# Retention scores of a chunk packed into three quarters of their block, with key halves swapped for every second head pair

## The chip, the cores and the metric

The kernel runs on one core of one Trainium2 chip. The metric is device time in microseconds, from three timed runs; beside them stands one profiled execution, whose trace the rows below come from.

## The reference

Decayed attention ("retention") over 4 batches of 8 heads, 576 tokens and head width 64, then two feed-forward layers (512 to 2048 to 512), the first with a leaky ReLU, the second with a squared ReLU:

```python
scores = scale * np.matmul(q, k.transpose(0, 1, 3, 2))
gamma = 1.0 - 2.0 ** (-5.0 - np.arange(H, dtype=np.float32))
rel = pos[:, None] - pos[None, :]
Dmat = np.where(rel >= 0, gamma[:, None, None] ** rel[None, :, :], 0.0)
ret = scores * Dmat[None, :, :, :]
x = np.matmul(ret, v)              # -> (B*S, H*D)
h = x @ w_in;  g = np.maximum(0.01 * h, h);  x = g @ w_out      # first layer
h = np.maximum(x @ w_in, 0.0);  out = h * h @ w_out             # second layer
```

A score whose key comes after its query is multiplied by zero.

## The kernel before

The retention part cuts each batch into four chunks of 128 tokens and one of 64 (20 chunks, numbered 0 to 19; chunks 4, 9, 14 and 19 are the short ones, chunks 0, 5, 10 and 15 open a batch). Inside a chunk the scores are formed and multiplied with V; what earlier chunks contribute comes through a running state. For each chunk `i` the program writes, in this order on each engine's queue:

- `load` and `load_rows`: q, k transposed (`kt`), and k and v by rows (`kv`) come in through SyncE's DMA queue, four chunks ahead, into five buffers each.
- `scores` (L515), two chunks ahead of the output: for a full chunk 16 matmuls of 64 x 64 weights by 128 columns into PSUM `scps` (two buffers); then VectorE multiplies all 128 x 1024 numbers by the decay mask (L518) into `r`. Scores of chunk i+2 need the buffer that L518 of chunk i reads.
- `decay`: GpSimd scales q (L531) and k (L535).
- `output`: the state product (L549, from the second chunk of a batch on), the within-chunk product of `r` and v (L557, 8 matmuls of 128 rows by 128 columns), ScalarE's copy of `ops` into `ysb` (L560), the sums that update the state (L566), and ScalarE's copy of the sums into `state` (L570), which the next chunk's state product reads.

Between chunks, `run` and `build` put work for the feed-forward part into the same queues, by the written tables RATE and BUILD: VectorE and ScalarE unpack weights (`steps_in`, `steps_out`, L149 to L216) and prepare the operands of the first layer (`operands`, L256 to L281). Into the last three chunks go the first products of that layer (L318). Behind the retention part the feed-forward layers follow, with matmuls of 128 x 128 weights by 384 or 512 columns (L318, L419), and VectorE and ScalarE beside them. All orders are written by hand (`manual_schedule`); each engine works through its queue in order.

Of the kernel before, what the change touches and what calls it, by code (L numbers as in the profile page):

```python
# [10 lines left out]
F32 = mybir.dt.float32  # L11
F32R = mybir.dt.float32r
U32 = mybir.dt.uint32
AF = mybir.ActivationFunctionType
# [3 lines left out]
B, H, S, D = 4, 8, 576, 64  # L18
NT, DM, DFF = B * S, H * D, 2048
P = 128  # L20
NP = H // 2
# [5 lines left out]
HT = 384  # L27
NB = NT // (2 * HT)
FULL = S // P
C = NP * P  # L30
# [12 lines left out]
AHEAD = 2  # L43
# [7 lines left out]
def retention_ffn_kernel(ctx: ExitStack, tc: tile.TileContext, full, rows, half, halfv, w1, w2, const, mask, gk, out):  # L51
# [12 lines left out]
    nc = tc.nc  # L64
    sub, mul, add, mx = ALU.subtract, ALU.mult, ALU.add, ALU.max
# [7 lines left out]
    ysb = [keep.tile([P, NK * 2 * HT], F32, name=f"ysb{i}") for i in range(NB)]  # L73
# [32 lines left out]
    class Weights:  # L106


        def __init__(self):
            self.tasks = []  # L110
            for g in range(2 * NG):
                layer, f = divmod(g * GRP, NF)
                a, b, c, d = ((j, layer, f + 2 * u) for j in range(2) for u in range(NU))

                self.tasks += [a, c, d, b] if g else [a, b, c, d]
            self.raws, self.loads = [], 0
            self.clock, self.due, self.arrive = 0, 0, 0
            self.free, self.later = False, True
# [320 lines left out]
    def halves_of(t0, n):  # L439
        for i in range(2 * NB):  # L440
            a, z = max(t0, i * HT), min(t0 + n, (i + 1) * HT)
            if a < z:
                yield i, a, z

    def tokens(i):
        b, c = chunks[i]
        return b * S + c * P, P if c < FULL else S - FULL * P

    class Retention:
        def __init__(self, pool, outputs):  # L450
# [52 lines left out]
        def scores(self, i):  # L503

            q, k = self.raw[i][:2]
            n = tokens(i)[1]

            ps = wide(i % 2, "scps").rearrange("p j (a t) -> p j a t", t=P)
            for p in range(NP):
                c = slice(p * n, (p + 1) * n)  # L510
                for f in range(0, n, D):
                    for j in range(2):
                        s = slice(j * D, (j + 1) * D)
                        o = slice(f, f + D) if n == P else s
                        nc.tensor.matmul(ps[o, j, p, :n], k[s, c][:, f : f + D], q[s, c], start=True, stop=True, skip_group_check=True)  # L515
# [4 lines left out]
            for j in range(2):  # L520
                s = slice(j * D, (j + 1) * D)
                nc.vector.tensor_tensor(t[s, j, :, :n], ps[s, j, :, :n], self.mask[s, j, :, j * D : j * D + n], mul)

        def decay(self, i):

# [6 lines left out]
            if c < FULL:  # L532
                k = kv[:, 0, :].rearrange("p (h e) -> p h e", e=D)
                g = self.gk[:, c].unsqueeze(2).to_broadcast([P, H, D])
                nc.gpsimd.tensor_tensor(k, k, g, mul)  # L535

        def output(self, i):
            q, _, kv = self.raw.pop(i)
            rs = self.r.pop(i)
            t0, n = tokens(i)  # L540
            c = chunks[i][1]
            ops = self.ops[:, :, i % 2]
            for p in range(0, NP if c > 0 else 0, 2):
# [6 lines left out]
            for p in range(0, NP, 2):  # L550
                for e in range(4):
                    j, h = e // 2, e % 2
                    a = p + h
                    s = slice((2 * a + j) * D, (2 * a + j + 1) * D)
                    o = ops[h * D : (h + 1) * D, j, p // 2, :n]
                    f = slice(0, P) if n == P else slice(j * D, (j + 1) * D)
                    nc.tensor.matmul(o, kv[f, 1, s], rs[f, j, a, :n], start=(c == 0 and p == 0), stop=(p == NP - 2), skip_group_check=True)  # L557
            for i, a, z in halves_of(t0, n):
                x = ysb[i // 2].rearrange("p (j s t n) -> p j s t n", j=2, s=2, t=2)[:, :, :, i % 2, a - i * HT : z - i * HT]
                nc.scalar.activation(x, ops[:, :, :, a - t0 : z - t0], AF.Copy)  # L560
            if c < FULL:

                for p in range(NP):
                    for j in range(2):
                        s = slice((2 * p + j) * D, (2 * p + j + 1) * D)
                        nc.tensor.matmul(  # L566
                            self.sums[j * D : (j + 1) * D, p], kv[:, 0, s], kv[:, 1, s],
                            start=(c == 0 and p == 0), stop=(c == FULL - 1 and p == NP - 1), skip_group_check=True,
                        )
                nc.scalar.activation(self.state, self.sums, AF.Copy)  # L570


    weights = Weights()
# [26 lines left out]
    with tc.manual_schedule():  # L600
        with tc.tile_pool(name="att", bufs=1) as pool, tc.tile_pool(name="outputs", bufs=1, space=PSUM) as outputs:
            att.append(Retention(pool, outputs))
            ret = att[0]
            n = len(chunks)
# [19 lines left out]
            for i in range(n):  # L624
# [15 lines left out]
                a, t = tokens(i)  # L640
# [81 lines left out]
def constants():  # L722

    gamma = (1.0 - 2.0 ** (-5.0 - np.arange(H, dtype=np.float32))).astype(np.float64)
    scale = 1 / np.sqrt(D)
    row, col = np.arange(P)[:, None], np.arange(C)[None, :]
    gq = [gamma[row // D + 2 * (col // P)] ** (c * P + col % P) * scale for c in range(1, FULL + 1)]
    since = col % P - row
    mask = [np.where(since >= 0, gamma[2 * (col // P) + j] ** np.maximum(since, 0) * scale, 0) for j in range(2)]
    gk = gamma ** -(np.arange(FULL)[:, None] * P + row[:, :, None]).astype(np.float64)  # L730
    return [a.astype(np.float32) for a in (np.stack(gq), np.concatenate(mask, axis=1), gk.reshape(P, -1))]


# [45 lines left out]
```

## Time and profile before

| | |
|---|---|
| three timed runs | 842.29, 838.79, 840.78 us; median 840.78 us |
| the profiled execution | 841.1 us, of which 839.3 us span |
| busy in the span: TensorE, VectorE, ScalarE, GpSimd | 813.3, 603.4, 333.4, 44.4 us |
| mean granted TensorE clock | 0.992 |

The span runs from the first to the last instruction; the time of an execution also holds what lies around it, 1.8 us here. An engine's busy time overlaps with that of the others. GpSimd works in the retention part only.

### The profile page before, as it was taken

To read this page: it belongs to the slowest core of one execution; us is meant where nothing else is said; L and a number is where in the kernel's file an instruction comes from. 1 tells how busy PE (TensorE), PEld (TensorE's weight loads), DVE (VectorE), ACT (ScalarE), POOL (GpSimd) and SP (SyncE) were. 2 spreads that over 40 slices of the span, in tenths; PEclk is the share of its full clock that TensorE was granted. 3 is DMA by queue.
4 is the path that set the end of the run, shared out by engine and by line. 5 is a ranking of instruction groups with operands and counts; after the bars stand their busy time and mean duration, and the time that the engine had idled before them with its cause. 6 is when DMAs were issued, how large, how long until landed. Compare 5 with 4: busy or idle time off the path is not lost.

```text
span 839.3 us, 13140 instructions
## 1 busy us (share of the span) xinstructions
PE 813.3 (97%) x5468; PEld 767.1 (91%) x5468; DVE 603.4 (72%) x737; ACT 333.4 (40%) x431; POOL 44.4 (5%) x36
## 2 busy tenths in 40 slices
PE   7887999999999999999999999999999999999998
PEld 6777899999999999999999998998998998998996
DVE  4897889657666566658668879868778778754534
ACT  1344656544523433524525365443422333321211
POOL 3853000000000000000000000000000000000000
PEclk9998999999999999999999999999999999999999
DMA  9987473966656737746823554966855756745711
GB/s 360 393 311 278 150 276 121 420 244 243 259 175 243 255 135 288 263 134 243 302 99 132 182 226 164 390 246 228 299 174 205 265 169 243 263 145 193 289 51 75
DMA packets 45947, 191.58 MB, mean 228 GB/s; under 512 B 5696, under 2 KB 6720, under 8 KB 45888
## 3 DMA queue, kind: packets, MB, share of 16 engines
q1 hardware_dynamic: 45456, 189.96, 60.9%
q8 instruction: 43, 0.70, 0.3%
q10 hardware_dynamic: 432, 0.79, 0.3%
q14 instruction: 16, 0.13, 0.0%
HBM read 152.98 MB, written 37.75 MB: 227 GB/s over the span
## 4 chain that ended last, share of the span: by engine, by line
PE 82%; DVE 8%; DMA 5%; ACT 2%; issue 2%; SPq 0%; ACTq 0%; DVEq 0%
PE yps L419 44%; PE a L318 21%; PE b L318 15%; DMA kt<-in_full 2%; DMA raw<-in_w 1%; DMA gq<-in_const 1%; ACT sf L149 1%; DMA kv<-in_rows 1%; DVE sf L205 1%; DVE ilo L187 1%; PE ops L557 1%; DVE x L260 1%; DVE r L518 1%; DVE t L370 0%; DVE sf L209 0%
## 5 line engine op out<-in xcount | busy, mean ns | idle before, releaser
L318 PE MATMUL a<-x,ihi 128*128 128x384 f32 x768 | 196.0, 336 | 2.8 <-DVE t L384 2.5
L318 PE MATMUL b<-x,ihi 128*128 128x384 f32 x576 | 146.5, 335 | 0.8 <-DVE t L370 0.8
L318 PEld LDWEIGHTS a<-x,ihi 128*128 128x128 f32 x768 | 138.4, 188 | 5.9 <-DVE t L384 4.0
L419 PE MATMUL yps<-ghi,ohi 128*128 128x384 f32 x384 | 128.6, 335 | 1.0 <-ACT ysb L428 1.0
L318 PE MATMUL a<-x,ilo 128*128 128x384 f32 x384 | 128.5, 335 | 0.0
L419 PE MATMUL yps<-ghi,olo 128*128 128x384 f32 x384 | 128.3, 334 | 0.0
L419 PE MATMUL yps<-glo,ohi 128*128 128x384 f32 x384 | 128.3, 334 | 0.0
L356 DVE TENSOR_TENSOR glo<-t,ghi 128x768 fp32r<-128x768 f32 x96 | 91.7, 956 | 45.8 <-ACT ghi L351 45.2
L430 DVE TENSOR_TENSOR ysb<-yps,ysb 128x384 f32<-128x384 f32 (+1 forms) x126 | 76.1, 611 | 61.2 <-PE yps L419 60.9
L419 PE MATMUL yps<-ohi,glo 128*128 128x512 f32 x288 | 112.3, 390 | 0.0
L419 PE MATMUL yps<-olo,ghi 128*128 128x512 f32 x288 | 112.3, 390 | 0.0
L419 PE MATMUL yps<-ohi,ghi 128*128 128x512 f32 x288 | 112.0, 389 | 0.0
L351 ACT ACTIVATE ghi<-t 128x768 fp32r<-128x768 f32 x96 | 81.1, 845 | 68.5 <-DVE t L329 55.1
L318 PEld LDWEIGHTS b<-x,ihi 128*128 128x128 f32 x576 | 103.7, 188 | 1.6 <-DVE t L370 1.1
L344 ACT ACTIVATE s<-a 128x768 f32<-128x768 f32 x47 | 38.2, 814 | 155.3 <-PE a L318 155.2
L318 PE MATMUL b<-x,ilo 128*128 128x384 f32 x288 | 96.3, 334 | 0.0
L419 PEld LDWEIGHTS yps<-ghi,ohi 128*128 128x128 f32 x384 | 72.1, 188 | 1.9 <-ACT ysb L428 1.3
L419 PEld LDWEIGHTS yps<-glo,ohi 128*128 128x128 f32 x384 | 72.1, 188 | 0.0
L419 PEld LDWEIGHTS yps<-ghi,olo 128*128 128x128 f32 x384 | 72.1, 188 | 0.0
L318 PEld LDWEIGHTS a<-x,ilo 128*128 128x128 f32 x384 | 72.1, 188 | 0.0
L419 PEld LDWEIGHTS yps<-ohi,glo 128*128 128x128 f32 x288 | 54.0, 188 | 11.3
L419 PEld LDWEIGHTS yps<-olo,ghi 128*128 128x128 f32 x288 | 54.0, 188 | 11.0
(67 smaller groups left out, 976.2 us busy)
## 6 DMA issues: line engine op xcount, KB each, us to landing
x<-x SPq DMA_DIRECT2D x168, 768.0 KB, 6.0
raw<-in_w SPq DMA_DIRECT2D x62, 512.0 KB, 5.9
kv<-in_rows SPq DMA_DIRECT2D x16, 512.0 KB, 6.0
out<-ysb SPq DMA_DIRECT2D x18, 256.0 KB, 2.0
q<-in_full SPq DMA_DIRECT2D x16, 256.0 KB, 5.2
kt<-in_full SPq DMA_DIRECT2D x13, 256.0 KB, 5.1
ysb<-in_w SPq DMA_DIRECT2D x2, 512.0 KB, 6.7
kv<-in_halfv SPq DMA_DIRECT2D x4, 256.0 KB, 5.6
```

Of the source, the lines that this page charges most:

```text
L149: nc.scalar.activation(f32(a), f32(raw[:, :, 1]), AF.Abs)
L187: nc.vector.tensor_tensor(lo[:, a:z], sf[:, a + 1 : z + 1], f32(hi[:, a:z]), sub)
L205: nc.vector.scalar_tensor_tensor(rest, high, 23, low, ALU.logical_shift_left, ALU.bitwise_or)
L260: nc.vector.tensor_tensor(t[:, 1], src, f32(t[:, 0]), sub)
L318: nc.tensor.matmul(ps[:, u, :HT], a[:, w, s], x[:, b, k], start=(start and k == 0 and i == 0), stop=(k == 1 and i == 2), skip_group_check= ...
L344: nc.scalar.activation(t, ps[:, :, :HT], AF.Copy)
L351: nc.scalar.activation(h, t, AF.Copy)
L356: nc.vector.tensor_tensor(l, t, f32(gs[key][0]), sub)
L419: nc.tensor.matmul(acc, a, b, start=(j == u == i == 0), stop=(j == 1 and u == NU - 1 and i == 2))
L430: nc.vector.tensor_tensor(y, acc, y, add)
L518: nc.vector.tensor_tensor(t, ps, self.mask, mul)
L557: nc.tensor.matmul(o, kv[f, 1, s], rs[f, j, a, :n], start=(c == 0 and p == 0), stop=(p == NP - 2), skip_group_check=True)
```

## The change

Of a chunk's 128 x 128 scores per head, the quarter of first-half queries by second-half keys is all zero after the mask. `scores` no longer multiplies it: keys of the first half meet all 128 queries (8 matmuls of 128 columns), keys of the second half only the 64 late ones (8 matmuls of 64 columns). So that three blocks of 64 columns hold two heads without a hole, every second head pair (`odd`) has its key halves swapped: its early keys stand in partitions 64 to 127. The host swaps the halves in `kv` alike, and mask and `gk` follow. The mask product is one VectorE operation on 128 x 768 numbers (L540), and a short chunk's mask is a tile of its own (`tail`), with a DMA of its own.

The within-chunk product falls into two: `within(1)`, late queries with all 128 keys (8 matmuls of 64 columns), and `within(0)`, early queries with 64 early keys (8 matmuls of 64 columns, of which even pairs use rows and output partitions 0 to 63 and odd pairs 64 to 127). `within(1)` stays ahead of the sums, `within(0)` goes behind them, and so does the copy of `ops` to `ysb`, which now follows the copy of the state. Ahead of either part a new matmul of 2 columns (`fence`) is put, in chunks that are neither the first nor the last of a batch.

```diff
-            self.mask = pool.tile([P, 2, NP, P], F32, name="mask")
+            self.mask = pool.tile([P, 2, NP // 2, 3 * D], F32, name="mask")
+            self.tail = pool.tile([P, NP, D], F32, name="tail")
...
-            nc.sync.dma_start(self.mask.rearrange("p j a t -> p (j a t)"), mask)
+            nc.sync.dma_start(self.mask.rearrange("p j a t -> p (j a t)"), mask[:, : -C // 2])
+            nc.sync.dma_start(self.tail.rearrange("p a t -> p (a t)"), mask[:, -C // 2 :])
...
-            t = self.r[i] = self.pool.tile([P, 2, NP, P], F32, tag="r", bufs=1 + AHEAD, name="r")
-            if n == P:
-                nc.vector.tensor_tensor(t, ps, self.mask, mul)
...
+            for a in range(NP // 2):
+                for late in range(2):
+                    for j in range(2):
+                        s = slice(j * D, (j + 1) * D)
+                        for odd in (late, 1 - late):
+
+                            c = (2 * a + odd) * P
+                            f = (late ^ odd) * D
+                            o = ps[f : f + D, j, a, 1 + odd] if late else ps[f : f + D, j, a, : 2 + odd : 1 + odd]
+                            x = q[s, c + late * D : c + P].rearrange("p (b t) -> p b t", t=D)
+                            nc.tensor.matmul(
+                                o, k[s, c + late * D : c + late * D + D], x[:, 0] if late else x,
+                                start=True, stop=True, skip_group_check=True,
+                            )
+            m = self.mask.rearrange("p j a c -> p j (a c)")
+            t, ps = (x.rearrange("p j a b t -> p j (a b t)") for x in (t, ps))
+            nc.vector.tensor_tensor(t, ps, m, mul)
...
+        def fence(self):
+
+            ps = bank("fence", 3)
+            nc.tensor.matmul(ps[:D, :2], self.cold[:D, :D], self.cold[:D, :2], start=True, stop=True)
...
-                    nc.tensor.matmul(o, kv[f, 1, s], rs[f, j, a, :n], start=(c == 0 and p == 0), stop=(p == NP - 2), skip_group_check=True)
-            for i, a, z in halves_of(t0, n):
-                x = ysb[i // 2].rearrange("p (j s t n) -> p j s t n", j=2, s=2, t=2)[:, :, :, i % 2, a - i * HT : z - i * HT]
-                nc.scalar.activation(x, ops[:, :, :, a - t0 : z - t0], AF.Copy)
+
+            def within(part):
+                for a in range(NP // 2):
+                    for e in range(4):
...
+                        elif part:
+                            f = slice(0, P)
+                            x, o = rs[:, j, (3 * a + 1 + h) * D : (3 * a + 2 + h) * D], o[:, D:]
+                        else:
+                            f = slice(h * D, (h + 1) * D)
+                            x, o = rs[f, j, 3 * a * D : (3 * a + 1) * D], o[:, :D]
...
+            if 0 < c < FULL:
+                self.fence()
+            within(1)
             if c < FULL:
...
                 nc.scalar.activation(self.state, self.sums, AF.Copy)
+                if c > 0:
+                    self.fence()
+                within(0)
+            for i, a, z in halves_of(t0, n):
+                x = ysb[i // 2].rearrange("p (j s t n) -> p j s t n", j=2, s=2, t=2)[:, :, :, i % 2, a - i * HT : z - i * HT]
+                nc.scalar.activation(x, ops[:, :, :, a - t0 : z - t0], AF.Copy)
```

TensorE's queue at chunk 18, the last full one, before the change: state product, within-chunk product, sums, and the first products of the feed-forward part (`a`, `b`).

```order
L549 MATMUL ops<-q,state 64x128 x8
L557 MATMUL ops<-r,kv 64x128 x8
L566 MATMUL sums<-kv 64x64 x8
L318 MATMUL b<-x,ihi 128x384 x2
L318 MATMUL b<-x,ilo 128x384
```

The same place after the change (L572 is the state product, L590 the two parts of the within-chunk product, L600 the sums):

```order
L572 MATMUL ops<-q,state 64x128 x8
L558 MATMUL fence<-cold 64x2
L590 MATMUL ops<-r,kv 64x64 x8
L600 MATMUL sums<-kv 64x64 x8
L558 MATMUL fence<-cold 64x2
L590 MATMUL ops<-r,kv 64x64 x8
L318 MATMUL b<-x,ihi 128x384 x2
L318 MATMUL b<-x,ilo 128x384
```

Two fences have come in, and half of the within-chunk product stands behind the sums.

ScalarE's queue around chunks 14 to 16 before the change: the copies of chunk 14 (64 columns), the weight step L212, then the copies of chunk 15 (`ysb`, `state`) and of chunk 16.

```order
L560 ACTIVATE ysb_68<-ops 128x4x64
L212 ACTIVATE ohi<-sf 128x1024
L560 ACTIVATE ysb_68<-ops 128x4x128
L570 ACTIVATE state<-sums 128x256
L560 ACTIVATE ysb_68<-ops 128x4x64 x2
L570 ACTIVATE state<-sums 128x256
```

And after the change:

```order
L610 ACTIVATE ysb_68<-ops 128x4x64
L212 ACTIVATE ohi<-sf 128x1024
L604 ACTIVATE state<-sums 128x256
L610 ACTIVATE ysb_68<-ops 128x4x128
L604 ACTIVATE state<-sums 128x256
L610 ACTIVATE ysb_68<-ops 128x4x64 x2
```

In each full chunk the copy of the state now stands ahead of the copy of the output. VectorE's, GpSimd's and SyncE's queues keep their order, but for the DMA of `tail` behind that of `mask`.

## Rows read from the trace of the kernel before

**Rows 1.** Busy time by stretch: engines in us, TensorE's granted clock, DMA share, GB/s.

```profile
0.00:35.30 35.30, 26.21 (x560) 23.07 (x562) 22.37 (x22) 9.96 (x16) 18.47 (x17) 0.95 0.98 380
35.30:71.70 36.40, 27.90 (x692) 24.78 (x690) 36.11 (x34) 13.56 (x25) 24.16 (x18) 0.91 0.82 286
71.70:85.60 13.90, 13.90 (x217) 12.35 (x217) 8.10 (x10) 7.34 (x13) 1.80 (x3) 0.86 0.89 350
85.60:130.00 44.40, 42.01 (x237) 40.12 (x234) 37.90 (x46) 27.42 (x38) 0.00 (x0) 1.00 0.52 190
130.00:839.30 709.30, 703.26 (x3777) 666.75 (x3775) 498.95 (x628) 275.15 (x339) 0.00 (x0) 1.00 0.59 218
```

**Rows 2.** Chain that ended last, from 20 to 75 us: start, us, what.

```profile
23.74 7.27 DMA kt<-in_full
...
34.08 1.20 ACT sf L149
...
68.55 1.14 DVE sf L209
...
70.68 0.58 ACT ysb L560
71.26 0.28 ACT state L570
...
71.68 1.13 PE ops L549 x16
```

**Rows 3.** TensorE's waits up to 86 us: total, times, longest.

```profile
PE scps L515 <- DVE r L518: 6.5, 4, 2.6
```

**Rows 4.** VectorE's groups by line and shape: count, busy us, mean ns, idle before.

```profile
L370 DVE TENSOR_TENSOR t<-b,s 128x768 f32<-128x768 f32 x24 | 23.0, 956 | 55.5 <-PE b L318 55.4
...
L518 DVE TENSOR_TENSOR r<-scps,mask 128x1024 f32<-128x1024 f32 x16 | 19.3, 1214 | 7.1 <-DMA mask<-in_mask 5.3 <-PE scps L515 1.8
...
L207 DVE TENSOR_SCALAR sf<-sf 128x1024 uint32<-128x1024 uint32 x16 | 12.0, 753 | 0.0
```

**Rows 5.** VectorE in order of time, 33 to 75 us: start, us, what.

```profile
36.53 1.21 DVE L518 TENSOR_TENSOR r<-scps,mask 128x1024 f32<-128x1024 f32 x1
...
65.66 1.76 DVE L207 TENSOR_SCALAR sf<-sf 128x1024 uint32<-128x1024 uint32 x1
67.34 1.21 DVE L518 TENSOR_TENSOR r<-scps,mask 128x1024 f32<-128x1024 f32 x1
```

**Rows 6.** TensorE in order of time, 19 to 23 us.

```profile
19.18 1.10 PE L515 MATMUL scps<-q,kt 64*64 64x128 f32 x32
20.11 0.62 PE L549 MATMUL ops<-q,state 64*64 64x128 f32 x16
20.66 1.09 PE L557 MATMUL ops<-r,kv 128*64 128x128 f32 x16
21.58 0.63 PE L566 MATMUL sums<-kv 128*64 128x64 f32 x16
22.14 0.68 PE L515 MATMUL scps<-q,kt 64*64 64x64 f32 x16
```

**Rows 7.** TensorE in order of time, 43 to 45 us.

```profile
44.13 0.41 PE L549 MATMUL ops<-q,state 64*64 64x64 f32 x16
```

**Rows 8.** Waits of TensorE's weight loads, 13 to 86 us: total, times, longest.

```profile
PEld ops L557 <- issue: 2.7, 14, 0.3
```

**Rows 9.** TensorE in order of time, from 71 us.

```profile
72.74 1.97 PE L557 MATMUL ops<-r,kv 128*64 128x128 f32 x16
74.50 1.07 PE L566 MATMUL sums<-kv 128*64 128x64 f32 x16
```

**Rows 10.** ScalarE in order of time, from 65 us.

```profile
82.31 0.60 ACT L560 ACTIVATE ysb<-ops 128x512 f32<-128x512 f32 x1 [0.77 <-PE ops L557]
...
83.11 1.57 ACT L256 ACTIVATE x<-ysb 128x768 fp32r<-128x768 f32 x2
```

**Rows 11.** TensorE's waits, 85 to 480 us: total, times, longest.

```profile
PE b L318 <- DVE t L370: 0.8, 1, 0.8
```

More of the change, by code (lines that the diff above doesn't have):

```diff
@@ L506, in scores @@
             n = tokens(i)[1]
[L508 to L511, printed above, removed]
+            ps = wide(i % 2, "scps")
+            t = self.r[i] = self.pool.tile([P, 2, NP // 2 * 3 * D], F32, tag="r", bufs=1 + AHEAD, name="r")
+            if n < P:
+                ps, t = (x[:, :, : NP * n].rearrange("p j (a t) -> p j a t", t=n) for x in (ps, t))
+                for p in range(NP):
+                    c = slice(p * n, (p + 1) * n)
@@ L520, in scores @@
-            for j in range(2):
-                s = slice(j * D, (j + 1) * D)
-                nc.vector.tensor_tensor(t[s, j, :, :n], ps[s, j, :, :n], self.mask[s, j, :, j * D : j * D + n], mul)
+                        nc.tensor.matmul(ps[s, j, p], k[s, c], q[s, c], start=True, stop=True, skip_group_check=True)
+                for j in range(2):
+                    s = slice(j * D, (j + 1) * D)
+                    nc.vector.tensor_tensor(t[s, j], ps[s, j], self.tail[s], mul)
+                return
@@ L549, in output @@
                     nc.tensor.matmul(o, self.state[s, a], q[s, a * n : (a + 1) * n], start=(p == 0), stop=False, skip_group_check=True)
[L550 to L556, printed above, removed]
-                    nc.tensor.matmul(o, kv[f, 1, s], rs[f, j, a, :n], start=(c == 0 and p == 0), stop=(p == NP - 2), skip_group_check=True)
-            for i, a, z in halves_of(t0, n):
-                x = ysb[i // 2].rearrange("p (j s t n) -> p j s t n", j=2, s=2, t=2)[:, :, :, i % 2, a - i * HT : z - i * HT]
-                nc.scalar.activation(x, ops[:, :, :, a - t0 : z - t0], AF.Copy)
+            def within(part):
+                for a in range(NP // 2):
+                    for e in range(4):
+                        j, h = e // 2, e % 2
+                        s = slice((4 * a + 2 * h + j) * D, (4 * a + 2 * h + j + 1) * D)
+                        o = ops[h * D : (h + 1) * D, j, a]
+                        if n < P:
+                            f = slice(j * D, (j + 1) * D)
+                            x, o = rs[f, j, (2 * a + h) * D : (2 * a + h + 1) * D], o[:, :n]
+                        elif part:
[4 more added lines that the diff above has]
+                            x, o = rs[f, j, 3 * a * D : (3 * a + 1) * D], o[:, :D]
+                        first = c == 0 and a == 0 and part == 1
+                        nc.tensor.matmul(o, kv[f, 1, s], x, start=first, stop=(a == NP // 2 - 1), skip_group_check=True)
+            if 0 < c < FULL:
+                self.fence()
+            within(1)
             if c < FULL:
@@ L727, in constants, with decay @@
     gq = [gamma[row // D + 2 * (col // P)] ** (c * P + col % P) * scale for c in range(1, FULL + 1)]
-    since = col % P - row
-    mask = [np.where(since >= 0, gamma[2 * (col // P) + j] ** np.maximum(since, 0) * scale, 0) for j in range(2)]
-    gk = gamma ** -(np.arange(FULL)[:, None] * P + row[:, :, None]).astype(np.float64)
+    head = np.arange(H)
+    key = (row + (head // 2 % 2) * D) % P
+    def decay(since, h):
+        return np.where(since >= 0, gamma[h] ** np.maximum(since, 0) * scale, 0)
+    t = np.arange(D)
+    mask = []
+    for j in range(2):
+        for a in range(NP // 2):
+            for b in range(3):
+                odd = row // D if b == 0 else b - 1
+                h = 2 * (2 * a + odd) + j
+                k = (row + odd * D) % P
+                mask.append(decay(t + (b > 0) * D - k, h))
+    for p in range(NP):
+        mask.append(decay(t - row % D, 2 * p + row // D))
+    gk = gamma ** -(np.arange(FULL)[:, None] * P + key[:, None, :]).astype(np.float64)
     return [a.astype(np.float32) for a in (np.stack(gq), np.concatenate(mask, axis=1), gk.reshape(P, -1))]
@@ L739, with halves_turned @@
     n = FULL * P
+    def halves_turned(a):
+        a = a.reshape(-1, 2, D, NP // 2, 2, P).copy()
+        a[:, :, :, :, 1] = a[:, ::-1, :, :, 1]
+        return a.reshape(-1, P, DM)
     def turned(a, sl, c):
@@ L750 @@
     full = np.stack([turned(q, s0, FULL), turned(k, s0, FULL)], axis=1)
-    kv = np.stack([rows(k, s0, FULL), rows(v, s0, FULL)], axis=2)
+    kv = np.stack([halves_turned(rows(x, s0, FULL)) for x in (k, v)], axis=2)
     half = np.stack([turned(q, s1, 1), turned(k, s1, 1)], axis=1)
```

5 lines of the change are left out of this document (3 added, 2 removed).

## The prediction

> **What bounds the kernel now.** I read the busy time by stretch first [rows 1]. From 130 us on TensorE is busy for 703.26 of 709.30 us. Nothing of the change lies there, so that part can only be shifted as a whole. What can be won or lost is when the feed-forward part gets going, and three stretches decide it.
>
> Up to 35.3 us the DMA share is 0.98 while TensorE is busy for 26.2 us. The chain has a transfer of `kt` of 7.27 us there [rows 2]: the loads set the pace. From 35.3 to 71.7 us VectorE is busy for 36.11 of 36.40 us. TensorE waits 6.5 us for its mask product L518 [rows 3], and the chain runs through VectorE to the weight step L209 at 68.55 us, from there over ScalarE (L212, `ysb`, `state`) to TensorE's state product of chunk 16 at 71.68 us [rows 2]. From 71.7 to 85.6 us TensorE has no gap (13.90 of 13.90). After that TensorE and VectorE are nearly balanced up to 130 us; TensorE waits 0.8 us for L370 [rows 11].
>
> So a saving on VectorE counts in the second stretch, a cost on TensorE in the third, and TensorE's savings in the first two lie beside a wait for DMA or VectorE.
>
> **First stretch: about 0.** The mask's bytes are the same in two DMAs; all loads together still go through engines with a share of 0.98. The issue of one more DMA is covered by that; if it weren't, it would cost one issue. The saved score quarter lies here beside the waits for `kt`. One thing leaks out: ScalarE's weight step L149 at 34.08 us, from which VectorE's chain starts [rows 2], stands behind the `ysb` copy of chunk 5, and that copy now waits for `within(0)`. Before, scores and within-chunk product took 0.93 + 1.09 us (start to start, and the length of the last, [rows 6]). After, they take 0.72 (scores, below) + 0.51 + 0.56 + 0.68 us. That is 0.45 later for `ysb`, less the 0.28 [rows 2] that the state copy no longer stands between it and L149: **+0.2 us**.
>
> **VectorE: the mask product on 768 instead of 1024 numbers.** L518 takes 1214 ns. L370 has just the form that L540 will have (PSUM by SBUF, two banks of 384 columns) and takes 956 ns [rows 4]. That is 0.258 us for each of 16, but only those between 35.3 us and L209 count: seven, the first at 36.53 and the last at 67.34 us [rows 5], or 1.81 us. Not all of it comes through. GpSimd is busy for 24.16 us of the stretch [rows 1], two thirds, and VectorE's other operations are slow beside it: one L207 takes 1.76 us where the mean is 0.75 [rows 4, 5]. L518 takes 1.21 us in either case. If two thirds of the freed time now holds operations that run at some 0.6 of their speed, 0.66 x 0.4 x 1.81 = 0.48 us is lost. Ends: 1.81 and 1.33; I take **-1.35 us**.
>
> **ScalarE: the state copy ahead of `ysb`.** Behind L212 the chain has `ysb` 0.58 us, then `state` [rows 2]. With the order turned, the state product of chunk 16 starts earlier by that time. **-0.5 us** (ends 0.4 and 0.58). So that product should start at 71.68 + 0.2 - 1.35 - 0.5 = 70.0 us.
>
> **TensorE: matmuls.** Start to start, scores take 0.93, state product 0.55, within-chunk product 0.92, sums 0.56 us [rows 6]. Eight matmuls on four 64 x 64 tiles take 0.62 us with 128 columns [rows 6] and 0.41 with 64 [rows 7]; the late half of the scores so saves 0.21: 0.72. This is hidden, as chunks 16 to 18 have no full scores behind them.
>
> `within(1)` has 8 matmuls of 64 columns in the form of the sums, so between half of 0.92 and 0.56 us: 0.51. `within(0)` uses two of the four 64 x 64 tiles, as the short chunk's scores do, which are 0.68 us long [rows 6]: start to start between 0.46 and 0.68, again 0.51. So nothing is saved in the within-chunk product: two parts of 0.51 for one of 0.92, +0.1. The zeros left out were streamed through half of the rows; leaving out rows saves no columns.
>
> **The fences.** No row shows a matmul of 2 columns. Below, it slips into its neighbours' time: 0. Above, it empties the array: the 0.41 us of eight short matmuls less the 0.21 that 64 columns take leave 0.20 us of drain [rows 7], and a weight load after a change of tile shape stands idle for 2.7 / 14 = 0.19 us [rows 8]: together 0.39. In tile shape it is like one of its two neighbours, and it waits for an earlier user of its bank only, so I take 0.1, near the lower end. There are 24 fences, but only the six in chunks 16 to 18 lie on the path.
>
> **Third stretch.** Chunk 16 runs at the lower of the two clock levels, 1.2 GHz: its within-chunk product takes 1.76 us start to start [rows 9], 1.9 times the 0.92 above. (0.1 + 2 x 0.1) x 1.9 = **+0.55 us**. Chunk 17: 0.1 + 0.2 = 0.3, and `within(0)` is in another tile shape than the sums before it and L318 behind it, one change more than before: 0.1 by [rows 8], less what is in the fence; **+0.4 us**. In chunk 18 what counts is the copy `ysb` at 82.31 us and L256 at 83.11 [rows 10], on which VectorE's and then TensorE's wait for L370 rests [rows 11]. `ysb` waited for the within-chunk product, 1.09 us [rows 6]. Now it waits for 0.1 + 0.51 + 0.56 + 0.1 + 0.68 = 1.95, 0.86 later; the state copy no longer stands between it and L256, 0.2 back: **+0.65 us**.
>
> The Trainium skill, "TensorEngine Tiling (Array Packing)", Key Properties, says that a change of the tiling mode drains the engine. The trace agrees in kind: the idle 0.19 us stands at each such change. Taken as a full drain, the change in chunk 17 would cost 0.39 instead of 0.1, and the sum below would be 0.3 higher.
>
> **The sum.** 0.2 - 1.35 - 0.5 + 0.55 + 0.4 + 0.65 = -0.05 us on the profiled execution's 841.1 us (839.3 of span and 1.8 around it). That execution is 0.3 us above the median of the timed runs, so I expect a median of 840.7 us. What VectorE saves, TensorE gives back in the last three full chunks. A measurement of this kernel can tell about 0.5% from no change, 4.2 us.
>
> **Ends of the sum.** With no fence, no extra in the within parts, and VectorE's full 1.81: 0.2 - 1.81 - 0.58 + 0 + 0 + 0.2 = -2.0. With 0.39 for a fence and 0.2 more for the within parts: 0.2 - 1.33 - 0.4 + (0.3 + 0.78) x 1.9 + (0.3 + 0.78 + 0.1) + 1.2 = +2.9.
>
> **Rivals.**
> *Fences that drain.* The upper end: about 843.6 us. For it: they stand where results that follow in the same bank are still on their way. Against it: the idle 0.19 us of [rows 8] is all that a change of tile shape costs now. Still no change that can be told.
>
> *The clock falls elsewhere.* The mean granted clock of the third stretch, 0.86 [rows 1], is 3.9 of 13.9 us at half, 71.7 to 75.6 us. TensorE's waits for L518, up to 2.6 us long [rows 3], lie ahead of it, and they become shorter. If it stays at 2.4 GHz, the state product (1.06 to 0.55), the within-chunk product (1.76 to 0.92) and the sums (1.07 to 0.63 long) of chunk 16 give back 1.8 us [rows 2, 6, 9]: 838.9.
>
> *Faster by more than 4.2 us.* All 16 mask products would have to count, 16 x 0.258 = 4.1, with ScalarE's 0.5 and the clock's 1.8, less the 1.6 on TensorE: 4.8, so 836.0. Against it: 0.98 DMA share in the first stretch, where five of them lie.
>
> *Slower by more than 4.2 us.* `within(0)` keeps half of the array idle and the fences nearly all of it, and the low clock of chunk 16 goes on through chunks 17 and 18. All of the 10 us from 75.6 to 85.6 us, dense matmuls, would take up to twice as long. It decides from about 4.5 us more of low clock on; lasting to 85.6 us it gives up to 850. Against it: in the trace the clock came back after 3.9 us, with the same kind of work before it.
>
> That the change doesn't do what it says: score matmuls with two pieces of 64 columns might cost more than 0.72; there TensorE waits anyway, up to 6.5 us, so 840.7 remains.
>
> **How the numbers follow.** Sum as worked out, 838.7 to 842.0: 0.57, with 0.02 for costlier scores. Draining fences, 842 to 843.6: 0.13. Clock back early: 0.12. Faster: 0.07. Slower: 0.09. Same is then 0.84. The likeliest gives 840.7. The range takes in the early clock and the draining fences, 837.5 to 844.0, and leaves out faster and slower, 0.16.
>
> **What would show it.** L540 at 0.96 us; the state product of chunk 16 starting at about 70.0 us; from there to the end of the retention part some 1.5 us more than the 13.9 us before; TensorE's wait for the mask product shorter; from 130 us on the same 709 us. The prediction is wrong if the low clock moves by several us, if a fence takes over 0.4 us, or if the first 35 us change their length.

## The result and the profile after

The changed kernel takes **845.98 us** in the median of 5 runs (845.45 to 847.04); the kernel before, run beside it, 838.79. The ratio is **1.0068**, 95% interval 1.0049 to 1.0086: slower by 0.7%. (The quotient of the two medians is 1.0086, the upper end of that interval; this text goes by the ratio.) The prediction was 840.7 us, no change that can be told, with a range of 837.5 to 844.0. It was wrong.

The profiled execution takes 847.04 us, 845.3 of it span, 5.9 more than the one before. Busy time by stretch, columns as in [rows 1] (start and end, length, busy time of TensorE, of its weight loads, of VectorE, ScalarE and GpSimd with their numbers of instructions, granted clock, DMA share, GB/s), with a short stretch as its last row:

```profile
0.00:35.30 35.30, 27.87 (x600) 25.79 (x600) 19.58 (x21) 9.14 (x15) 15.33 (x16) 0.85 0.98 370
35.30:71.70 36.40, 30.49 (x885) 28.28 (x886) 32.42 (x34) 13.11 (x24) 23.18 (x17) 0.91 0.85 291
71.70:85.60 13.90, 8.87 (x163) 8.23 (x163) 8.77 (x10) 5.96 (x11) 6.38 (x5) 0.88 0.69 251
85.60:130.00 44.40, 43.01 (x323) 41.07 (x323) 35.34 (x43) 26.53 (x39) 0.00 (x0) 1.00 0.56 206
82.00:85.70 3.70, 3.70 (x28) 3.56 (x27) 1.01 (x2) 2.44 (x4) 0.00 (x0) 0.54 0.22 91
```

From 71.7 to 85.6 us TensorE was busy without a gap before (13.90 of 13.90, [rows 1]). Now it is busy for 8.87. In the second stretch VectorE has some room now (busy for 32.42 of 36.40 us instead of 36.11). What TensorE (PE in the rows; DVE is VectorE, ACT ScalarE, POOL GpSimd) waits for instead, up to 95 us (total, times, longest):

```profile
PE sums L600 <- issue: 5.0, 2, 3.1
PE scps L534 <- issue: 3.8, 3, 1.3
PE scps L534 <- DVE ilo L187: 2.2, 1, 2.2
...
PE ops L572 <- ACT ysb L610: 1.3, 3, 0.5
```

The same view of the kernel before has two rows of that kind:

```profile
PE sums L566 <- issue: 0.5, 2, 0.4
PE scps L515 <- issue: 0.3, 1, 0.3
```

"Issue" is time in which the engine waited for nothing that the profile shows. It has grown from 0.8 to 8.8 us, and the 6.5 us that the scores waited for the mask product [rows 3] are gone. TensorE in order of time shows that these gaps fall into groups of equal matmuls, where the program has no wait:

```profile
57.91 0.34 PE L600 MATMUL sums<-kv 128*64 128x64 f32 x4 [1.95 <-issue]
...
70.52 0.89 PE L534 MATMUL scps<-q,kt 64*64 64x128 f32 x29
72.75 0.33 PE L534 MATMUL scps<-q,kt 64*64 64x64 f32 x3 [1.35 <-issue]
73.59 0.67 PE L572 MATMUL ops<-q,state 64*64 64x128 f32 x16 [0.51 <-ACT ysb L610]
74.05 0.22 PE L558 MATMUL fence<-cold 64*64 64x2 f32 x2
74.20 0.69 PE L590 MATMUL ops<-r,kv 128*64 128x64 f32 x16
...
78.06 0.40 PE L600 MATMUL sums<-kv 128*64 128x64 f32 x6
81.53 0.56 PE L600 MATMUL sums<-kv 128*64 128x64 f32 x10 [3.08 <-issue]
...
83.20 1.01 PE L318 MATMUL a<-x,ihi 128*128 128x384 f32 x2
```

The sums of chunk 17 stop for 3.08 us after six of sixteen records. At 73.59 us stands the state product of chunk 16, which I had put at 70.0. Behind the long gap the granted clock is at the lower level, 1.2 GHz (0.54 from 82.0 to 85.7 us), and the first products L318 run slowly. The mask product itself came out as forecast, 950 ns (L370 956):

```profile
L540 DVE TENSOR_TENSOR r<-scps,mask 128x768 f32<-128x768 f32 x16 | 15.1, 950 | 9.9 <-PE scps L534 9.8
```

**Where the gaps stand.** I numbered the instructions of TensorE's queue in the order of the trace; a matmul of the retention part stands there as two weight loads and two matmuls. The five gaps for issue stand at 961, 1985, 2241, 3009 and 3265, all 193 beyond a multiple of 256, and so does the wait put down to L187, at 1217. The three small gaps before stand at 1217, 1473 and 1729, the same remainder. The page of the changed kernel has a queue that carries instructions; its columns are packets, MB and share:

```profile
q8 instruction: 45, 0.74, 0.3%
```

That is 16.4 KB a packet, and 45 packets for 11,700 recorded instructions: 260 a packet. Before they are 43 for 11,097. Laid beside TensorE's times, the packets in the trace's records look like this (us):

```
          TensorE at n-256   packet starts   landed   TensorE at n-1   at n
after
 n= 961        25.91             28.95        29.91        29.57       31.18
 n=1985        46.97             49.35        50.28        50.26       51.62
 n=2241        51.62             55.69        56.62        55.74       57.91
 n=2497        57.91             60.28        61.20        63.49       63.50
 n=3009        67.73             70.42        71.39        71.19       72.75
 n=3265        72.75             79.16        80.29        78.23       81.53
before
 n=1217        31.81             35.13        36.05        36.90       37.37
 n=1729        42.82             45.31        46.27        47.10       47.47
```

A packet starts 2.4 to 6.4 us after TensorE has come to the instruction 256 ahead, takes about 1 us, and in each gap TensorE goes on 1.2 to 1.4 us after it has landed. The 256 instructions between last 3.3 to 4.1 us in the first four gaps after the change; before, 4.3 to 5.1 us. So the reading is: TensorE's program is fetched in pieces of 256 instructions, and the changed kernel uses a piece up before the next is there. Eight matmuls and two fences more in a middle chunk are 40 instructions more (four each), 200 instead of 160. The fifth gap, the longest, is of another kind: its 256 instructions last 5.5 us (72.75 to 78.23), longer than any of the three before the change, but the packet starts 6.4 us after its turn. Here it is the late packet more than the denser stream.

### The profile page after: what moved, and what is told of

The parts are those of the page before. It is cut to its first block, busy times and chain, and to the rows that moved or that the text cites. A ratio compares the mean times of both kernels' runs of the same rounds, so it can differ in the third digit from the quotient of the medians.

```text
span 845.3 us, 13745 instructions
## 1 busy us (share of the span) xinstructions
PE 818.9 (97%) x5772; PEld 774.9 (92%) x5772; DVE 599.9 (71%) x737; ACT 334.2 (40%) x431; POOL 44.9 (5%) x36
## 4 chain that ended last, share of the span: by engine, by line
PE 85%; DVE 6%; issue 3%; ACT 3%; DMA 2%; SPq 0%; DVEq 0%; ACTq 0%
PE yps L419 44%; PE a L318 21%; PE b L318 15%; PE ops L590 2%; DMA raw<-in_w 1%; ACT sf L149 1%; PE ops L572 1%; PE sums L600 1%; PE scps L534 1%; DVE ilo L187 1%; DMA ysb<-in_w 1%; DVE sf L205 1%; DVE x L260 0%; DVE t L370 0%; DMA kt<-in_full 0%
## 5 line engine op out<-in xcount | busy, mean ns | idle before, releaser
L318 PE MATMUL a<-x,ihi 128*128 128x384 f32 x768 | 196.9, 337 | 2.7 <-DVE t L384 2.4
L318 PE MATMUL b<-x,ihi 128*128 128x384 f32 x576 | 146.5, 335 | 0.9 <-DVE t L370 0.9
L318 PEld LDWEIGHTS a<-x,ihi 128*128 128x128 f32 x768 | 139.1, 189 | 5.9 <-DVE t L384 4.0
L318 PE MATMUL a<-x,ilo 128*128 128x384 f32 x384 | 128.9, 336 | 0.0
L318 PEld LDWEIGHTS b<-x,ihi 128*128 128x128 f32 x576 | 103.7, 188 | 1.8 <-DVE t L370 1.2
L318 PE MATMUL b<-x,ilo 128*128 128x384 f32 x288 | 96.3, 334 | 0.0
L318 PEld LDWEIGHTS a<-x,ilo 128*128 128x128 f32 x384 | 72.4, 188 | 0.0
```

What stands on the lines that cost most here:

```text
L318: nc.tensor.matmul(ps[:, u, :HT], a[:, w, s], x[:, b, k], start=(start and k == 0 and i == 0), stop=(k == 1 and i == 2), skip_group_check= ...
```

## The experiments

Theory 1 is this supply of instructions; theory 2, the added matmuls' own time on TensorE; theory 3, the state product that waits for the copy to `ysb`. Ratios are to the kernel before on the same chip, its medians 840.7 to 841.0 us; a run's difference to before is worked out from its ratio, 0.1% being 0.84 us.

**1. As many matmuls in the kernel before.**

```diff
                 nc.scalar.activation(self.state, self.sums, AF.Copy)
+                ps = bank("fill", 3)
+                for _ in range(10 if c > 0 else 8):
+                    nc.tensor.matmul(ps[:D, :2], self.cold[:D, :D], self.cold[:D, :2], start=True, stop=True)
```

> The kernel before, and behind each copy of the state ten matmuls of 64 x 64 weights by 2 columns (eight in the first chunk of a batch), whose result nobody reads: 152 in all, as many matmuls as the change adds, and nothing else of the change. Theory 1 (instruction supply: TensorE's program comes in packets of 256 instructions, and the denser stream runs out of them): idle stretches of TensorE that wait for nothing but issue, of 1 to 3 us each, appear in the retention part, 0.8 us in all before, 3 to 9 us now; time 842 to 846 us against 838.8. Theory 2 (the added matmuls' own time on TensorE): at most 0.05 us each, 0.5 per chunk, hidden beside the waits for VectorE but for the last three full chunks: +1.5 us, 840.3, and no idle stretch for issue above 0.5 us.

847.94 us, ratio 1.0088 (1.0060 to 1.0116), slower than I expected and than the change. TensorE's waits for issue:

```profile
PE sums L566 <- issue: 3.9, 2, 2.4
...
PE fill L573 <- issue: 1.2, 1, 1.2
```

Gaps of 1.2, 1.5 and 2.4 us are there, at instructions 1217, 2241 and 3265, without packed scores, a cut product or another order of copies. But theory 2's bound was too low: ten such matmuls take 1.08 us from start to start (40.89 to 41.97 us), 0.11 each. So this run shows that more instructions alone bring the gaps, but not that the gaps alone bring the time. In its profiled execution the part from the state product of chunk 16 (75.50 us) to the end of the retention part (96.70) takes 21.2 us instead of 13.9. Of these 7.3 us the gap is 2.4; the added matmuls' own time in three chunks is 3.2, at 1.08 each; and the granted clock is at its lower level from 84.1 to 91.0 us (0.51). Own time counts here at least as much as the gap.

**2. Fewer instructions in the kernel before.**

```diff
-                        o = slice(f, f + D) if n == P else s
-                        nc.tensor.matmul(ps[o, j, p, :n], k[s, c][:, f : f + D], q[s, c], start=True, stop=True, skip_group_check=True)
+                    o = slice(0, P) if n == P else s
+                    nc.tensor.matmul(ps[o, j, p, :n], k[s, c], q[s, c], start=True, stop=True, skip_group_check=True)
```

> The kernel before with the scores of a full chunk as 8 matmuls of 64 x 128 weights by 128 columns instead of 16 of 64 x 64 weights: the same products, 32 TensorE instructions fewer per full chunk of about 160. Theory 1: the 0.8 us of idle for issue in the retention part goes to about 0; time 838.0, 0.3 to 0.9 us less than before, if VectorE doesn't take it all. Theory 2: what counts is columns streamed, which are the same for each part of the array; time as before, 838.8 within 0.5, and the idle for issue stays.

839.48 us, ratio 0.9986 (0.9971 to 1.0001): 1.2 us less, at the edge of what the interval allows. No wait for issue is left up to 95 us. The wide scores take 1.09 us from start to start where the sixteen narrow ones take 0.92 to 0.93, so it isn't columns that gained. Of the kernels that leave nothing out it is the fastest here, but not told apart from the one before.

**3. The gain on VectorE alone.**

```diff
-                nc.vector.tensor_tensor(t, ps, self.mask, mul)
+                t, ps, m = (x.rearrange("p j a t -> p j (a t)")[:, :, : NP * 96] for x in (t, ps, self.mask))
+                nc.vector.tensor_tensor(t, ps, m, mul)
```

> The kernel before with the mask product on 768 instead of 1024 columns (a quarter of the masked scores is left out, and the within-chunk product reads other columns of the same tile instead): the change's gain on VectorE without anything on TensorE. The prediction's term: 0.96 instead of 1.21 us for each mask product, state product of chunk 16 earlier by 1.3 to 1.8 us, time -1.35 us, 837.4. Theory 1 (TensorE runs out of instructions): TensorE's waits for VectorE become shorter and part of the gain comes back as idle for issue; the state product of chunk 16 earlier by 0.3 to 1.3 us, 837.5 to 838.5. Were the gain on VectorE worth nothing here, 838.8.

839.21 us, ratio 0.9987 (0.9973 to 1.0002): 1.1 us less. The state product of chunk 16 starts at 69.60 instead of 71.68 us, 2.1 earlier, more than the upper end of my term. More than half of it is lost again by the end of the retention part (84.77 instead of 85.59 us), 0.61 us in a new gap for issue:

```profile
69.60 1.13 PE L550 MATMUL ops<-q,state 64*64 64x128 f32 x16 [1.63 <-ACT state L571]
...
77.18 0.33 PE L567 MATMUL sums<-kv 128*64 128x64 f32 x2 [0.61 <-issue]
```

**4, 9, 10, 11. The limits of 256 moved.** Both kernels got matmuls of 2 columns at the start, beside the wait for the first loads: 32, 16 and 48 in the changed kernel (runs 4, 9, 10), 32 in the one before (run 11).

```diff
             ret.keep_warm(WARM[0])
+            ret.shift(32)
...
+        def shift(self, n):
+            ps = bank("shift", 3)
+            for _ in range(n):
+                nc.tensor.matmul(ps[:D, :2], self.cold[:D, :D], self.cold[:D, :2], start=True, stop=True)
```

> The changed kernel with 32 matmuls of 2 columns (128 TensorE instructions) ahead of everything, beside the wait for the first loads. After the change TensorE's idle stretches for issue stand at TensorE's instructions 961, 1217, 1985, 2241, 3009 and 3265, all 193 beyond a multiple of 256. Theory 1: they stay at numbers with that remainder and so move by 128 instructions to other places of the program; their sum stays of the order of 9 us (5 to 11), the time 843 to 849. A rival, that it is luck where the limits of 256 fall: the sum falls below 3 us and the time to 841. Theory 2 (the work at those places itself): the same lines idle at the same places of the program as before the shift, 846.

> The changed kernel with 16 matmuls of 2 columns (64 TensorE instructions) ahead of everything. Theory 1, with what the shift by 128 showed (idle for issue 8.4 us, none of it behind the state product of chunk 16, and 842.1 us): idle for issue counts in full only behind that product, where TensorE has no other wait. The limit that fell into the sums of chunk 17 now falls 64 instructions earlier, still in chunk 17: idle for issue of 1 to 3 us there, time 844 to 847. If the place doesn't matter, 842 to 849 for every shift with no relation to it.

> The changed kernel with 48 matmuls of 2 columns (192 TensorE instructions) ahead of everything. Theory 1: the limit of the last packet but one falls to the state product of chunk 16 or just behind it, the next one among the long matmuls of the feed-forward part; no idle for issue above 0.5 us behind the state product of chunk 16, and 841 to 843.

> The kernel before with 32 matmuls of 2 columns (128 TensorE instructions) ahead of everything. Theory 1: 256 instructions of this kernel last longer (4.6 to 5.6 us between 32 and 47 us) than their packet takes to come, so the place of the limits matters little: idle for issue below 2 us in all, time within 2 us of before. If such a shift by itself costs or gives as much as after the change (3.4 us), the place of the limits is as good a reason as the number of instructions.

| shift, instructions | changed kernel: us, ratio | kernel before: us, ratio |
|---|---|---|
| 0 | 845.98, 1.0068 (1.0049 to 1.0086) | 1 |
| 64 | 850.20, 1.0109 (1.0087 to 1.0132) | |
| 128 | 842.08, 1.0031 (1.0014 to 1.0047) | 841.50, 1.0015 (0.9993 to 1.0036) |
| 192 | 845.78, 1.0052 (1.0033 to 1.0071) | |

In every run the gaps stand at the same remainder, whatever line that is. With 128 more instructions:

```profile
27.78 0.57 PE L596 MATMUL ops<-r,kv 128*64 128x64 f32 x12 [1.95 <-issue]
...
55.17 0.61 PE L540 MATMUL scps<-q,kt 64*64 64x64 f32 x18 [3.59 <-issue]
70.04 0.27 PE L596 MATMUL ops<-r,kv 128*64 128x64 f32 x1 [1.37 <-issue]
```

With two smaller ones they sum to 8.4 us, close to the 8.8 after the change, but the last is ahead of the state product of chunk 16, and nearly half of the loss is gone by the ratios. With 64 more, the last one cuts the state product of chunk 17 in two, as long as the change's own last gap:

```profile
58.40 0.32 PE L578 MATMUL ops<-q,state 64*64 64x128 f32 x1 [3.45 <-issue]
82.47 0.70 PE L578 MATMUL ops<-q,state 64*64 64x128 f32 x8 [3.43 <-issue]
```

The place is the one forecast, the length (1 to 3 us) and the time (844 to 847) were not; this is the slowest kernel. The run with 192 missed too: its profiled execution, at 841.63 us the fastest of its twelve, has a gap of 0.89 us at 79.16, where I had expected none, and the others go up to 848.49. What differs between its executions no trace here shows. So where the limits fall is worth 6.6 us between the fastest and the slowest place by their ratios, but each of the four places is slower than before. In the kernel before the shift brings 2.0 us of idle for issue, ahead of 37 us, and nothing that can be told in the time.

**5, 6. Fewer loads.** The full chunks of batches two to four use the rows of the first batch again, in both kernels:

```diff
+            if b > 0 and c < FULL:
+                self.raw[i] += (self.kvs[c],)
+                return
```

> The kernel before without the loads of k and v by rows for the full chunks of the second to fourth batch (12 of 512 KB): those chunks use the rows of the first batch again, which GpSimd scales once more each time, so the numbers are others. Pair with the next run, which tells the theories apart by the difference of the two. By itself: DMA share before 86 us falls, the loads no longer hold up the first 35 us; 3 to 8 us less than before, 831 to 836.

> The changed kernel without the same loads. After the change the packets of TensorE's program start 1.4 to 6.4 us after TensorE has come to the packet before, beside DMA shares of 0.8 to 1. Theory 1: with the DMA engines less busy they start within about 1 us, and the idle for issue, 8.9 us in the retention part after the change, falls below 3 us; the difference to the kernel before with the same loads left out is -1 to +2 us, where it was +5.7. Theory 2 (the added matmuls' own time): the difference stays at +4 to +6 us, though the idle for issue is gone.

Before with fewer loads 837.63 us, ratio 0.9968 (0.9948 to 0.9988); changed 841.48, ratio 1.0009 (0.9992 to 1.0026). The DMA share from 35.3 to 71.7 us falls from 0.85 to 0.57, the packets that start in that stretch do so 1.2 to 2.0 us after their turn, one 4.2, where it was 1.4 to 4.1 (the next, whose turn is at 67.58 us, starts only 8.2 us later), and idle for issue falls from 8.8 to 3.5 us. The difference of the two kernels falls from 5.7 to 3.5 us by the ratios, less than theory 1 forecast (at most 2). In the profiled executions it is 1.85 us; these lie above the medians of their kernels, the one of before by 3.3 us and the changed one by 1.3, which makes up the rest. In the changed one the state product of chunk 16 starts at 70.19 us, 1.6 earlier than in its partner, where it waits for GpSimd's scaling of q:

```profile
70.19 1.13 PE L576 MATMUL ops<-q,state 64*64 64x128 f32 x16 [2.38 <-ACT ysb L614]
```

```profile
71.80 1.13 PE L553 MATMUL ops<-q,state 64*64 64x128 f32 x16 [1.97 <-POOL q L535]
```

**7. The order of before.**

```diff
             within(1)
             if c < FULL:
+                if c > 0:
+                    self.fence()
+                within(0)
+            for i, a, z in halves_of(t0, n):
+                x = ysb[i // 2].rearrange("p (j s t n) -> p j s t n", j=2, s=2, t=2)[:, :, :, i % 2, a - i * HT : z - i * HT]
+                nc.scalar.activation(x, ops[:, :, :, a - t0 : z - t0], AF.Copy)
+            if c < FULL:
...
                 nc.scalar.activation(self.state, self.sums, AF.Copy)
-                if c > 0:
-                    self.fence()
-                within(0)
-            for i, a, z in halves_of(t0, n):
...
```

> The changed kernel with the order of before: both parts of the within-chunk product, then the copy to ysb, then the sums and the copy of the state. As many instructions as the change. Theory 1: idle for issue at instruction numbers with the same remainder, 5 to 11 us in all, time 842 to 849. Theory 3 (the state product of the next chunk waits for the ysb copy, which the change put behind the second part at the chunk's end): TensorE's waits for ysb, three of 0.4 to 0.5 us after the change, are gone, and the time falls by 0.5 to 2 us, to 844.0 to 845.5; were it the whole cause, to 840.

844.88 us, ratio 1.0054 (1.0038 to 1.0071). The waits for `ysb` are gone from TensorE's waits; idle for issue is 8.2 us. The time is where theory 3 as a part of the cause put it, but against 1.0068 (1.0049 to 1.0086) it is no difference that can be told. Theory 3 is not the main cause; a part in it stays possible.

**8. The change without its packed scores.** Scores, mask product and weights as before; from `output` the parts of `within` (cut by columns), fences and order of copies as after the change.

```diff
-                    f = slice(0, P) if n == P else slice(j * D, (j + 1) * D)
-                    nc.tensor.matmul(o, kv[f, 1, s], rs[f, j, a, :n], start=(c == 0 and p == 0), stop=(p == NP - 2), skip_group_check=True)
+                        t = slice(part * D, (part + 1) * D) if n == P else slice(0, n)
+                        o = ops[h * D : (h + 1) * D, j, p // 2, t]
+                        nc.tensor.matmul(o, kv[f, 1, s], rs[f, j, a, t], start=first, stop=(p == NP - 2), skip_group_check=True)
```

> The kernel before (scores and mask product on 1024 columns) with the within-chunk product cut in two parts, the fences, the places of the sums and the order of copies of the change: the change without its packed scores, with as many TensorE instructions as the changed kernel. Theory 1: idle for issue as after the change, 4 to 11 us, time 843 to 849; the packing itself gives back 0 to 1.4 us between this run and the changed kernel. A rival, that the packed score matmuls are what is slow: no idle for issue above 1 us in all, and 841.

847.46 us, ratio 1.0076 (1.0054 to 1.0099), idle for issue 9.3 us. The packed scores are not what is slow: cutting the product, with its fences and its order, is enough. From here to the changed kernel it is 0.1%, less than the intervals.

**12. Packed scores from 12 matmuls.**

```diff
+                        o, w, x = (
+                            (ps[:, j, a, :2], slice(c, c + P), q[s, c : c + P].rearrange("p (b t) -> p b t", t=D)),
+                            (ps[:, j, a, 2], slice(d, d + P), q[s, d + D : d + P]),
+                            (ps[D:, j, a, 0], slice(d + D, d + P), q[s, d : d + D]),
+                        )[e]
```

> The changed kernel with the packed scores of a chunk from 12 matmuls instead of 16: of each two head pairs the even one with 64 x 128 weights by 128 columns, the odd one's late queries with 64 x 128 weights by 64 columns, and its early queries last, over the even one's zero quarter; the host swaps the key halves of the odd pairs in k transposed. The same output, 46 matmuls instead of 50 in a middle chunk. Theory 1: fewer instructions, less idle for issue, 2 to 7 us, and 841 to 845 us. If columns streamed counted (512 for each half of the array instead of 384), +0.2 us per chunk where TensorE is the limit, and 846 to 848.

845.28 us, ratio 1.0050 (1.0034 to 1.0066). Idle for issue falls to 2.6 us, but nothing is won: the scores take 1.46 us from start to start (61.33 to 62.79 us) instead of 1.07 (63.09 to 64.16 after the change), and TensorE is busy for 35.18 of the 36.40 us of the second stretch. Its one long gap stands where it costs most:

```profile
79.34 0.90 PE L597 MATMUL sums<-kv 128*64 128x64 f32 x10 [2.08 <-issue]
```

## Why the prediction was wrong, step by step

**The step that failed is the first.** "A cost on TensorE" was to count "in the third" stretch alone, and what the change does on TensorE in the first two was to lie "beside a wait for DMA or VectorE". After the change TensorE has little to spare there: with 5.8 us of gaps in which its program had not come, and more work of its own, it sets the pace for most of the two stretches. And in the third stretch I priced matmuls by their times in a stream that always had instructions, where a gap of 3.1 us now stands. The profile of before had a warning that I didn't read: 0.8 us of waits for issue in the middle of equal matmuls.

The profiled executions let the loss be divided. The retention part ends with the last short chunk, where the next L318 starts, in the kernel before and in the changed one:

```profile
85.59 0.62 PE L318 MATMUL a<-x,ihi 128*128 128x384 f32 x2
```

```profile
91.95 0.62 PE L318 MATMUL a<-x,ihi 128*128 128x384 f32 x2
```

That is 6.36 us later, in these parts:

- *Up to the state product of chunk 16:* 73.59 against 71.68 us, **+1.9**, where the terms gave -1.65. All of it is there already at the first step of VectorE's chain, L159, where I had +0.2 for the copy to `ysb` ahead of it. Before, then after:

```profile
35.30 1.30 DVE L159 TENSOR_SCALAR sf<-sf 128x1024 f32<-128x1024 f32 x1 [0.26 <-ACT sf L149]
```

```profile
37.20 1.47 DVE L159 TENSOR_SCALAR sf<-sf 128x1024 f32<-128x1024 f32 x1 [0.35 <-ACT sf L149]
```

  From there to the product both kernels take 36.4 us, so VectorE's gain did not come through either. The chain that ended last shows where it went. Before, it lay on a transfer of `kt` and then mostly on VectorE [rows 2]. After the change it lies on TensorE from 20 us, where the view starts, to 31.8, and again from 36.81 to 63.4, with gaps in it:

```profile
29.84 1.34 issue
...
50.47 1.15 issue
...
55.96 1.95 issue
...
63.91 1.17 ACT sf L149
```

  The scores that stop at 29.84 us hold up a mask product and with it VectorE's L187, for which ScalarE's L149 and so L159 wait. Gaps for issue of 5.8 us lie in front of the product; the last, 1.35 us, is not on this chain. Two other things lengthen TensorE's part. The granted clock is 0.50 from 18.0 to 24.1 us, where it was 1.00 before. And a middle chunk takes 3.28 us from state product to state product (64.16 to 67.44), where the times before make 2.96 and my terms 3.05: behind `within(0)` the packed scores take 1.07 us (66.37 to 67.44), not the 0.72 that I had, and more than the 0.93 of the unpacked ones. How the +1.9 divides among these three no run shows. With fewer loads, and so with fewer gaps, the same matmuls let L159 start at 35.87 and the product at 70.19 us, 34.3 us later, as in run 3 (35.42 and 69.60, 34.2): there VectorE's gain comes through.
- *From there on, TensorE's own work:* the changed kernel shifted by 128 and the kernel before shifted by 128 both run this part at full clock and without idle for issue. Busy time by stretch, the first row of run 4, the second of run 11, each from the state product of chunk 16 to the end of the retention part:

```profile
72.84:86.26 13.42, 13.03 (x276) 11.97 (x276) 9.25 (x11) 7.49 (x13) 4.52 (x4) 1.00 0.96 360
```

```profile
71.57:83.78 12.21, 12.16 (x216) 10.77 (x217) 8.92 (x11) 7.23 (x13) 2.58 (x3) 1.00 0.99 377
```

  13.42 less 12.21 is **+1.2** for three chunks. My terms had 0.3 for chunk 16 at this clock, 0.4 and 0.3 for the two others, 1.0. The size was about right; of what it is made not quite, since 0.39 us of it is a wait for `ysb` that no term had:

```profile
76.19 0.67 PE L578 MATMUL ops<-q,state 64*64 64x128 f32 x16 [0.39 <-ACT ysb L616]
```

- *The gap in the sums of chunk 17:* **+3.1**. Here nothing hides it.
- *The low clock:* 13.91 less 12.21 us is 1.7 before; after the change 18.36 from start to end, less 13.42 and 3.08, is 1.9: **+0.2**. It didn't go on, as a rival had it; it came at another place, behind the gap.

1.9 + 1.2 + 3.1 + 0.2 = 6.4. On the whole execution it is 5.9; the half microsecond given back later I didn't trace. The copy in chunk 18, for which I took 0.65 us, cost next to nothing: TensorE's wait for L370 is 0.9 us long instead of 0.8 [rows 11].

**VectorE's term** was too small: alone it brings the state product of chunk 16 forward by 2.1 us, not 1.35; the loss of speed to GpSimd that I took off did not show. After the change TensorE's pace used it up. **ScalarE's term** (-0.5) was wrong in kind. The state product is released by the copy to `ysb` of the chunk before, in runs 4 and 6 and after the change; before, it was the copy of the state that came last. Whichever stands last, the product waits for both, so their order gives nothing. Together they are off by 0.25 us, which is why the 70.19 us of run 6 look like a hit: that is luck.

**The fences** cost about what was taken, 0.1: it is 0.15 us from the first fence to the matmul behind it (74.05 to 74.20). The Trainium skill, "TensorEngine Tiling (Array Packing)", Key Properties, has a change of the tiling mode drain the engine; the 0.39 us that I had worked out for a full drain does not show there. Nor does the 0.19 us of [rows 8] stand at each change of tile shape, as I wrote: those waits are all ahead of the within-chunk product. **The rival** that the low clock goes on had the right sign for the wrong reason; the stretch that it counted from 71.7 us began at 68.9 already. And seven mask products, not five, lie in the first stretch; no term of the sum rests on that. No rival had TensorE waiting for its own program, and the range had no room for it.

What stays open: how much of the 3.5 us by which the pair with fewer loads still differs is gaps and how much TensorE's own work, why the packed scores take 1.07 us, and why run 10 spreads over 7 us.

## What to carry to other kernels

Count TensorE's instructions per microsecond, not only its columns: a change that cuts matmuls in two to save work elsewhere is paid where the program itself comes late. An engine that has time to spare before a change need not have it after: add up its new work and its gaps in the stretch where you call them hidden. Idle time "for issue" in the middle of a group of equal matmuls, at the same remainder of the instruction number, is the sign, and it stands in the profile of before at a tenth of the size. When such a kernel changes by some tenths of a per cent, shift its instruction numbers once or twice before believing that the edit did it.

## What the runs showed of the hardware

- TensorE's program arrives in packets of 16.4 KB, 256 instructions, on a queue of its own, which the page counts among those of the 16 DMA engines (0.74 MB, 45 packets). A packet started 0.4 us after its turn where the DMA share was 0.12 (before the change, turn at 69.11 us), 7.7 us at 0.77 (run 9, ahead of the gap at 82.47) and 8.2 us at 0.72 (run 6, turn at 67.58); ahead of the change's longest gap it was 6.4 us at 0.86, while three stores of `x` passed. Where TensorE stood in a gap for the packet, it went on 1.2 to 1.7 us after the landing.
- Behind the idle of 3.08 us after the change the granted clock fell to 0.54 for 3.7 us; behind 3.43 in run 9 it was 0.50 from 81 to 87 us; behind 1.53 in run 8 it stayed at 1.00. So the long gaps cost more than their own length. Against the kernel before this came to no more than the +0.2 us above, since there too the clock was 0.50 from 68.9 to 75.7 us, behind a wait of 2.17 us for the mask product.

```profile
81.00:87.00 6.00, 4.53 (x62) 4.28 (x63) 0.41 (x1) 0.90 (x3) 0.00 (x0) 0.50 0.61 251
```

```profile
81.00:86.00 5.00, 4.94 (x81) 4.52 (x82) 1.83 (x2) 3.26 (x5) 0.00 (x0) 1.00 0.58 238
```

  The first row is of run 9, the second of run 8; the clock is the third column from the end.
- A matmul of 64 x 64 weights by 2 columns takes 0.11 us back to back on one part of the array (run 1), though its columns are a sixty-fourth of those of a score matmul, of which sixteen, side by side on four parts of the array, take 0.93 [rows 6], 0.06 each.
